# Output products of two FFN batches by blocks, seven for eight, in a fused attention and FFN kernel

## The chip, the cores and the metric

The kernel runs on one core of a Trainium2 chip. The metric is the device time of one execution in microseconds (us), as the median of several runs. The engines are called PE (TensorE; PEld is its weight load), DVE (VectorE), ACT (ScalarE), POOL (GpSimd) and SP (SyncE, which issues DMAs). PSUM is the memory that PE writes its sums to; SBUF is the other one.

## The reference

Four batches, four heads, 1088 tokens, head size 32. The attention is linear, with features phi; what follows works on 4352 tokens of 128 values and is bilinear:

```python
def phi(x):
    a = np.einsum('rd,bhsd->bhsr', S1, x)
    b = np.einsum('rd,bhsd->bhsr', S2, x)
    return np.einsum('bhsi,bhsj->bhsij', a, b).reshape(*x.shape[:-1], r * r)
q_p, k_p = (phi(q), phi(k))
kv = np.einsum('bhsf,bhsd->bhfd', k_p, v)
z = np.sum(k_p, axis=2)
num = np.einsum('bhsf,bhfd->bhsd', q_p, kv)
den = np.einsum('bhsf,bhf->bhs', q_p, z)[..., None] + 1e-06
...
a = x @ w1          # x: 4352 x 128, w1 and w2: 128 x 1024
b = x @ w2
h = a * b @ w3      # w3: 1024 x 1024
return (h @ w_out).astype(np.float32)   # w_out: 1024 x 128
```

All of it is in f32 in the kernel; `w3 @ w_out` is multiplied out first (w3o, 1024 x 128), so that per token there are two products into 1024 values, an elementwise product, and one product back to 128.

## The kernel before, in words

The work is cut into named steps. `make_steps` defines a function for each, and the string `ORDER` (L71) lists their names; each engine gets its instructions in the order of that list, as `tile_polysketch_attn__then__multiplicative_ffn_kernel` chains every instruction to the one before it on its engine. Semaphore waits between engines follow from the data. Buffers are placed by hand as well: `SLOTS` (L28) gives, kind by kind, which of a few places each next tile takes; kind "b" are the eight banks of PSUM, kind "m" are SBUF tiles of 128 x 512. A tile that takes a place waits for the last reader of the tile that had it. The sets `POOL`, `ACTS`, `CPV` and `CPG` (L51 to L66) say which engine runs a step: `on(name)` is POOL, ACT or else DVE, `cp(name)` is a copy on DVE if the name is in `CPV` and else on ACT.

The tokens are worked in groups of 512 (`g0` to `g7`, two for each batch) and a rest of 256 (`gr`). For g0 to g3 and the rest, `ffn` (L1685) does for each of eight chunks c of 128 of the 1024 values: product a (`a`), its copy to SBUF (`c`), product b (`b`), their elementwise product on DVE (`m`), and the product with w3o that adds chunk c to the output (`o`, L1732, or L1721 for the rest). Then the output is transposed in blocks of 32 on DVE (`oT`), for g4 to g7 scaled (`oS`), and stored by four DMAs (`st`).

The last two batches (groups 4 and 5, 6 and 7) get their products a and b from `seven` (L1604), named h4 and h6: the 128 inputs are halved (rows lo and hi of the array), the 1024 outputs are halved (chunk i and chunk i + 4), and the tokens are halved (group g and group g + 1). That is a product of 2x2 blocks by 2x2 blocks, done with seven products for eight (Winograd's form). A product uses 64 rows and 128 columns of the array; the `a` of a product lies on the lower 64 rows, the `b` on the upper 64, so two of them run side by side. For each of four i and for a and b there are products 1 to 7 into PSUM tiles X, Y and Z (L1644), copies c, d, e, i (ACT, L1651), additions f, g, h (DVE, L1656), and four elementwise products m11, m12, m22 (DVE or POOL, L1678) and m21 (DVE, L1683). The step names are like `h4.2b7`: pair h4, i = 2, weight b, product 7. The four blocks of the result are `ab_sb[g, i]`, `ab_sb[g, i + 4]`, `ab_sb[g + 1, i]`, `ab_sb[g + 1, i + 4]`. The sums of x that `seven` needs are s1 to s4, those of the weights v.1 to v.4 (POOL). The product with w3o is plain for these groups: 8 products of 128x128 with 512 tokens for each group.

x itself comes from `q_wide` (L1301): step `q4.x` (and q6.x, qr.x for the rest) multiplies into four PSUM banks of 256 tokens each, one for each quarter t of the batch. `seven` needs each half of x's rows on both halves of SBUF, so step `xTt` (L1525) copies the two halves k of a bank to both places u, four copies of 64 x 256; the even quarters go to ACT, the odd ones to DVE:

```python
eng = act.copy if t % 2 == 0 else dve.tensor_copy
for k in range(2):
    for u in range(2):
        eng(xd[key, t // 2][k][u * 64:u * 64 + 64, t % 2 * W:t % 2 * W + W],
            s["x"][t][k * 64:k * 64 + 64, :W])
```

In time, the last third of PE's order is: products o of g0 to g3; qr.x and q6.x; h4 (with the first four products of h6); the 16 products o of g4 and g5, with some of the rest's a and b between them; h6; the 16 products o of g6 and g7, again with the rest's; the rest's last products; its output.

Of the kernel before, what the change touches and what calls it, by code (L numbers as in the profile page):

```python
# [23 lines left out]
KIND = {"b": "out h kvz t wa wb", "l": "ph kp cv_m cv_c kh pT w3c w3T wv", "m": "hc xd nz t2 qT q2 s_hl xT ffa ab ay_C oT",  # L24
# [37 lines left out]
    g0.1c g0.3c g2.1c g2.5c g2.6c g3.4c gr.1c gr.4c k0.kT1 k1.kvc k2.kT1 k2.kq k3.kT0 k3.kT1 k3.kq  # L62
    q0.xc0 q0.xc1
# [50 lines left out]
h4.0b6 h4.1ac h4.0be h4.0ad q6.xT2 q6.xT3 h4.s4 h4.s3 h4.0bh h4.0a7 h4.0ag h4.1b5 h4.0a2 h4.0b3 h4.0a3 h4.0b7 v.4
h4.0a4 h4.2b1 h4.1bd h4.1a6 h4.1b3 h4.0ai h4.1ae h4.0ah h4.2bc h4.1a5 h4.1ad h4.0bg h4.0m11 h4.0bf h4.0m22 h4.0af
h4.0b4 h4.1a2 h4.2b2 h4.1a7 h4.1b1 h4.0m21 h4.0m12 h4.2bh h4.1ah h4.1a3 h4.3b1 h4.2a1 h4.1ag h4.1af h4.1bc h4.1b6
h4.2a2 h4.2ac h4.2ah h4.2b6 h4.1a4 q4.ns h4.1be h4.1b2 h4.1bh h4.1bf h4.3a1 h4.1ai h4.3ac h4.2be h4.3bc h4.1b7 h4.2a6
h4.3b5 h4.3a5 h4.1bg h4.3b2 h4.1m12 h4.3bh h4.3ad h4.2ae h4.3a6 h4.3ae h4.1b4 h4.1m21 h4.1m11 h4.3a3 h4.2m11 h4.3b6
h4.2a5 h4.2b7 h4.3bd h4.3af h4.2a7 h4.2b5 h4.3be h4.2ad h4.2a3 h4.3b7 h4.2bd h4.2ag h4.3a7 h4.2bg h4.3b3 h4.2af h4.2a4
h4.2b3 h6.1a1 h6.s1 h4.3ag h4.2b4 h4.3bf h4.2ai h4.2m21 h4.3a4 h4.3bg h6.0b1 h4.3a2 h4.2m22 h4.2bf h4.3ai h6.1b1  # L120
h4.3ah h4.3m22 h6.0a5 h4.3b4 h4.3m21 g5.0o g4.0o g5.4o g5.1o g4.4o g4.1o g4.5o g4.2o gr.1a h4.2m12 h4.1m22 g5.5o g5.2o
g5.6o h4.3m11 h4.3m12 gr.0a gr.0c h6.0ad h6.1bc gr.1c h6.0bc g5.3o g5.7o g4.6o gr.1b g5.oT gr.1m g4.3o g4.7o gr.0b
g4.oT h6.s2 h6.1b2 h6.s3 gr.0m h6.s4 h6.1bh h6.1a2 h6.1ac h6.0b2 h6.1a6 h6.1b5 h6.1ae h6.0bh h6.0a1 h6.1ah h6.1b6
# [18 lines left out]
def make_steps(ctx, tc, q, k, v, S1, S2, moe_w1, moe_w2, moe_w3, moe_w_out, out):  # L142
# [6 lines left out]
    NC = DF // 128  # L149
# [257 lines left out]
    w12 = consts.tile([128, 2, 2, 512], F32, tag="w12")  # L407
# [1424 lines left out]
```

## Time and profile before

| | us |
|---|---|
| median of three runs | 249.13 |
| the three runs | 248.73, 249.13, 250.8 |
| span of the profiled execution | 250.57 |
| PE busy | 241.0 (96%) |
| DVE busy | 192.1 (77%) |
| POOL busy | 124.5 (50%) |
| ACT busy | 117.5 (47%) |
| first product of h4 | 158.51 |
| last product of the rest starts | 246.79 |

The profiled execution is one run of its own; its span is near the slowest of the three. A row of the profile gives a line of the kernel, the engine, the operation, the tiles written and read, and how often; behind it the busy time and the mean length of one in ns, then the idle time of the engine ahead of it and what ended that. In a timeline the first two numbers are the start from the span's start and the length, in us. PE's products are pipelined: a product's row is longer than the time after which the next one starts. An f32 product has two rows, one for each of its two passes. In the windows, a stretch of time has the busy time of each engine and, in brackets, its instructions.

### The profile page before, as it was taken

The numbers are of one execution on the slowest core, as the hardware profiler recorded it, in microseconds if no ns is written. First come the engines' busy times: TensorE is split into PE (matmuls) and PEld (weight loads), VectorE is DVE, ScalarE is ACT, GpSimd is POOL, SyncE is SP. The second block draws the span as 40 slices with busy tenths as digits, with TensorE's granted clock in tenths as the row PEclk, the third lists the DMA queues.
The fourth block names the chain that finished last, engine by engine and source line by source line (L and its number), as shares of the span: only waits on it lengthen the run. The fifth ranks groups of instructions, "written<-read, shape, count | busy, mean of one in ns | idle before, by whom it ended". The sixth has DMA issues, their size and how long they took to land.

```text
span 250.6 us, 6584 instructions
## 1 busy us (share of the span) xinstructions
PE 241.0 (96%) x2678; PEld 143.0 (57%) x2678; DVE 192.1 (77%) x402; ACT 117.5 (47%) x234; POOL 124.5 (50%) x180
## 2 busy tenths in 40 slices
PE   8978999999999999999999999999999999999994
PEld 5867555545454645966566544476444567645474
DVE  2874889989899979898999898878992158878051
ACT  3975875755985564394000140785610337530020
POOL 4485455635739589735579747835230063520010
PEclk9997999999999999999999999999999999999999
DMA  7582969787879977000000000460000004000004
GB/s 197 186 221 88 299 166 192 154 219 180 233 172 219 217 196 186 15 4 0 3 0 0 4 0 0 73 100 0 1 0 0 0 7 79 0 1 0 3 12 93
DMA packets 31934, 22.06 MB, mean 88 GB/s; under 512 B 21280, under 2 KB 26528, under 8 KB 31904
## 3 DMA queue, kind: packets, MB, share of 16 engines
q1 hardware_dynamic: 31360, 21.11, 35.1%
q8 instruction: 21, 0.34, 0.6%
q10 hardware_dynamic: 544, 0.52, 0.6%
q14 instruction: 9, 0.07, 0.1%
HBM read 19.40 MB, written 2.23 MB: 86 GB/s over the span
## 4 chain that ended last, share of the span: by engine, by line
PE 78%; DVE 11%; DMA 4%; issue 2%; SPq 2%; ACT 1%; POOL 1%; DVEq 0%; ACTq 0%
PE ps_o L1732 22%; PE ps_X L1644 11%; PE a_ps L1697 9%; PE b_ps L1707 8%; PE ps_w3o L526 6%; PE ps_Y L1644 6%; PE ps_Z L1644 3%; DMA kr<-in_k_dram 2%; PE ps_ac L1366 2%; DVE ab L1713 2%; PE ps_kv L761 2%; PE ps_x L1519 2%; DMA k<-in_k_dram 2%; PE ps_g L651 1%; PE ps_or L1721 1%
## 5 line engine op out<-in xcount | busy, mean ns | idle before, releaser
L1644 PE MATMUL ps_X<-xd,wv 64*128 64x512 f32 x112 | 43.0, 596 | 0.3 <-issue 0.3
L1707 PE MATMUL b_ps<-xT,w 128*128 128x512 f32 (+1 forms) x80 | 36.9, 560 | 0.3 <-DVE ab L1713 0.2
L1702 ACT COPY ffa<-a_ps 128x512 f32<-128x512 f32 (+1 forms) x32 | 16.9, 547 | 41.4 <-PE a_ps L1697 41.3
L1697 PE MATMUL a_ps<-xT,w 128*128 128x512 f32 (+1 forms) x80 | 35.9, 556 | 0.0
L1651 ACT COPY hc<-ps_X 128x512 f32<-128x512 f32 x40 | 22.0, 595 | 18.8 <-PE ps_X L1644 18.0
L1732 PE MATMUL ps_o<-hc,w3o 128*128 128x512 f32 x64 | 29.3, 595 | 0.0
L1732 PE MATMUL ps_o<-ab,w3o 128*128 128x512 f32 x64 | 29.1, 595 | 0.0
L1713 DVE TENSOR_TENSOR ab<-ffa,b_ps 128x512 f32<-128x512 f32 (+1 forms) x40 | 24.0, 621 | 3.8 <-PE b_ps L1707 3.3
L493 POOL TENSOR_TENSOR w3c<-w3c,cv_m 128x512 int32<-128x512 int32 x16 | 21.0, 1326 | 6.3 <-DVE w3c L487 6.3
L1644 PEld LDWEIGHTS ps_X<-xd,wv 64*128 64x128 f32 x112 | 18.8, 186 | 8.6 <-issue 3.4
L1697 PEld LDWEIGHTS a_ps<-xT,w 128*128 128x128 f32 x80 | 14.5, 190 | 15.9 <-issue 10.9
L1644 PE MATMUL ps_Y<-xd,wv 64*128 64x512 f32 x48 | 23.2, 595 | 0.0
L1707 PEld LDWEIGHTS b_ps<-xT,w 128*128 128x128 f32 x80 | 13.9, 190 | 13.7 <-issue 9.4
L1732 PEld LDWEIGHTS ps_o<-ab,w3o 128*128 128x128 f32 x64 | 11.8, 190 | 13.7 <-issue 13.0
L1732 PEld LDWEIGHTS ps_o<-hc,w3o 128*128 128x128 f32 x64 | 12.0, 190 | 12.4 <-issue 11.3
L1739 DVE STREAM_TRANSPOSE oT<-ps_o 128x512 f32<-128x512 f32 x8 | 5.7, 715 | 16.9 <-PE ps_o L1732 16.6
L526 PEld LDWEIGHTS ps_w3o<-wo,w3T 128*128 128x128 f32 x128 | 15.3, 192 | 3.2 <-issue 2.5
L526 PE MATMUL ps_w3o<-wo,w3T 128*128 128x128 f32 x128 | 15.9, 277 | 0.6 <-DVE w3T L520 0.6
L1678 POOL TENSOR_TENSOR hc<-hc 128x512 f32<-128x512 f32 x7 | 8.8, 1275 | 13.3 <-DVE hc L1656 11.8
L530 ACT COPY w3o<-ps_w3o 128x128 f32<-128x128 f32 x8 | 2.1, 272 | 26.2 <-PE ps_w3o L526 26.2
L255 ACT ACTIVATE cv_c<-raw 128x1024 f32<-128x1024 f32 (+1 forms) x13 | 13.1, 1017 | 1.4 <-DMA raw<-in_moe_w_dram 1.4
L1656 DVE TENSOR_TENSOR hc<-hc,ps_Y 128x512 f32<-128x512 f32 x16 | 10.7, 682 | 4.0 <-ACT hc L1651 2.8
(316 smaller groups left out, 527.8 us busy)
## 6 DMA issues: line engine op xcount, KB each, us to landing
raw<-in_moe_w_dram SPq DMA_DIRECT2D x32, 256.0 KB, 5.1
qh<-in_q_dram SPq DMA_DIRECT2D x4, 544.0 KB, 4.0
raw<-in_moe_w_dram SPq DMA_DIRECT2D x4, 512.0 KB, 5.6
out_dram<-oT SPq DMA_DIRECT2D x32, 64.0 KB, 1.9
k<-in_k_dram SPq DMA_DIRECT2D x3, 512.0 KB, 4.2
v<-in_v_dram SPq DMA_DIRECT2D x2, 512.0 KB, 6.2
kh<-in_k_dram SPq DMA_DIRECT2D x8, 128.0 KB, 3.0
raw<-in_moe_w_out_dram SPq DMA_DIRECT2D x4, 256.0 KB, 5.5
```

What stands on the lines that cost most here:

```text
L255: act.activation(dst, hi.bitcast(F32), ACT.Prelu, scale=2.0 ** -112, alpha=-2.0 ** 32)
L493: pool.tensor_tensor(d, d, x["m"][:, i * 512:(i + 1) * 512], ALU.add)
L526: pe.matmul(t["o"], w3T[ko][:, c], wo[:, c], start=c == 0, stop=c == NC - 1)
L1644: pe.matmul(x[bank], stat(j, u)[:, i * 128:(i + 1) * 128], rows(j, u), start=new, stop=True, tile_position=(u * 64, 0), skip_group_check=True)
L1651: act.copy(x[k], x[bank])
L1656: dve.tensor_add(x[k], x[k], x[bank])
L1678: on(f"h{g}.{i}m{k}").tensor_mul(both[0][k], both[0][k], both[1][k])
L1697: pe.matmul(x["a"][:, :w], w_of(0, c), xT[g][:, c0:c0 + w], start=True, stop=True)
L1702: cp(f"g{g}.{c}{su}c")(x["s"][:, :w], x["a"][:, :w])
L1707: pe.matmul(x["b"][:, :w], w_of(1, c), xT[g][:, c0:c0 + w], start=True, stop=True)
L1713: dve.tensor_mul(ab_sb[g, c][:, c0:c0 + w], x["s"][:, :w], x["b"][:, :w])
L1732: pe.matmul(o_ps[g], w3o[:, c], ab_sb[g, c], start=c == turn[0], stop=c == turn[-1])
```

## The change

Three parts.

The output products of g4 and g5, and of g6 and g7, are made by blocks too. In `seven`, behind the elementwise products, steps T1 to T4 form four differences of blocks of the result for each i (on DVE or POOL), steps P1 to P7 are seven products of 128 rows and 64 columns, with 512 tokens each, 28 for a pair, and steps k1 to k9 put the two groups' outputs together from four PSUM banks (k1 a copy, k2 to k9 additions on DVE). P1, P2 and P6 lie on the left 64 columns, P4, P5 and P7 on the right, P3 left for i = 0 and 1 and right for i = 2 and 3. Steps o.S1 to o.S4 form the sums of w3o that P3, P5, P6 and P7 use (`ws`, 128 x 256 each, POOL). The 32 plain products go.

A quarter of x is copied three times: `xTt` copies all 128 rows of the bank to one tile, `xSt` (two copies of 64 x 256) the halves crosswise to the other. The upper half of the array then has the other half of x in each product, and `stat`, v.1 to v.4 change the weights to match.

`ORDER` is new from about its last third on, with other engines for some steps: the copies c, d, e, i can go to DVE, and seven of them do. The rest's products a and b move mostly behind the last P; qr.p01 and qr.phi0 go from POOL to DVE. q6.x is now ahead of qr.x. The stores are ordered g0, g2, g1, g3 where they were g3, g2, g0, g1.

The core of the diff:

```diff
 POOL = set("""
-    g4.oS g5.oS g6.oS h4.0m11 h4.0m12 h4.2m22 h4.s1 h4.s3 h4.s4 h6.0m22 h6.1m12 h6.1m22 h6.3m22 h6.s1
...
+    g4.oS g5.oS g6.oS h4.0T2 h4.0T3 h4.0T4 h4.0m11 h4.0m12 h4.1T2 h4.1T3 h4.1m12 h4.1m22 h4.2T1
+    h4.2T2 h4.2T4 h4.2m11 h4.3T3 h4.s1 h4.s2 h4.s3 h6.0T1 h6.0T2 h6.0T3 h6.0m12 h6.1T1 h6.1T2 h6.1T4
+    h6.1m11 h6.1m12 h6.2T4 h6.2m11 h6.2m12 h6.2m22 h6.3T2 h6.3T4 h6.s2 h6.s3 h6.s4 k0.Nf k0.Nh k0.Nr
...
 CPV = set("""
-    g0.1c g0.3c g2.1c g2.5c g2.6c g3.4c gr.1c gr.4c k0.kT1 k1.kvc k2.kT1 k2.kq k3.kT0 k3.kT1 k3.kq
-    q0.xc0 q0.xc1
+    g0.1c g0.3c g2.1c g2.5c g2.6c g3.4c h4.0ad h4.0be h4.1ac h4.1ae h6.1ai h6.1bd h6.3bd k0.kT1
+    k1.kvc k2.kT1 k2.kq k3.kT0 k3.kT1 k3.kq q0.xc0 q0.xc1 q4.xS1 q4.xT0 q4.xT1 q4.xT2 q4.xT3 q6.xS0
+    q6.xS1 q6.xS2
...
 ORDER = """
-g2.2o qr.rc qr.bs qr.phi0 q6.pT0 g1.oT g2.1o g2.7o q6.pT1 g3.7o qr.pT0 h4.s1 g2.oT g3.oT qr.x v.2 qr.xT0 q6.x h4.0a1
-h4.s2 h4.0b1 h4.1a1 q6.xT0 q6.xT1 h4.0b5 h4.0ac h4.0bc g3.st g2.st g0.st g1.st h4.0a6 h4.0b2 h4.0a5 h4.0bd h4.0ae
+q6.x v.2 q6.xT0 qr.x qr.xT0 q6.xS0 h4.0a5 q6.xT2 h4.0b1 h4.s2 q6.xS2 h4.0bc h4.s3 h4.0a1 h4.0b2 h4.1a1 h4.1b1 h4.0ac
+q6.xT1 h4.0a6 q4.ns h4.1bc q6.xS1 h4.s4 h4.0bh h4.0ad h4.0ae h4.1ac h4.0b6 h4.0a2 h4.1b6 h4.0b5 v.4 h4.1a6 h4.0be
...
+h4.1T4 h4.3bf h4.3a3 h4.2m21 h6.3bc h4.0T2 h4.3a4 h4.3b4 gr.5a h4.3af h4.1P5 h4.1P6 h4.3bh
...
+h4.2T1 h4.2P5 h4.2P2 h4.3T2 h4.3T4 h4.0P1 h4.1P7 h4.0T4 h4.1P4 h4.3P1 h4.0P4 h4.2T2 h4.0P6 h4.2P6 h4.2T3 h6.s1 h4.3T3
...
+h4.2P3 h6.0b1 h6.0bc h6.0a5 h6.0ad h4.k3 h4.k2 h4.k4 h4.k5 h6.0b5 h4.k7 h4.k8 g3.st h4.k6 h6.0a6 h6.0ae h4.k9 h6.s4
...
+h6.3T2 h6.3T4 gr.5m h6.1P7 h6.3P2 h6.0P1 h6.3P5 h6.3P7 h6.3P1 h6.k1 h6.0T4 h6.3P4 h6.2T4 h6.1T4 h6.2P6 h6.0P4 h6.3P6
+h6.k2 q6.ns h6.0P3 gr.6m h6.k3 h6.k4 h6.k5 h6.k7 h6.1P4 h6.2P4 h6.1P3 gr.1a gr.6o0 gr.1b gr.0a gr.5o0 gr.6o1 gr.1c
...
@@ q_wide
-                    eng = act.copy if t % 2 == 0 else dve.tensor_copy
+                    cp(nm(f"xT{t}"))(quarter(xd[key, t // 2][0], t % 2), s["x"][t][:, :W])
+
+                @step(nm(f"xS{t}"))
+                def _(t=t):
                     for k in range(2):
-                        for u in range(2):
-                            eng(xd[key, t // 2][k][u * 64:u * 64 + 64, t % 2 * W:t % 2 * W + W],
-                                s["x"][t][k * 64:k * 64 + 64, :W])
+                        cp(nm(f"xS{t}"))(quarter(xd[key, t // 2][1], t % 2)[64 - k * 64:128 - k * 64],
+                                         s["x"][t][k * 64:k * 64 + 64, :W])
...
@@ seven
-                        act.copy(x[k], x[bank])
+                        cp(n(y))(x[k], x[bank])
...
+        B11, B12, B21, B22 = (lambda i, t=t, c=c: ab_sb[g + t, i + c] for t, c in ((0, 0), (1, 0), (0, 4), (1, 4)))
...
+                on(f"h{g}.{i}T1").tensor_sub(y[1, i], B12(i), B11(i))
...
+                on(f"h{g}.{i}T2").tensor_sub(y[2, i], B22(i), y[1, i])
...
+                on(f"h{g}.{i}T3").tensor_sub(y[3, i], B22(i), y[3, i])
...
+                on(f"h{g}.{i}T4").tensor_sub(y[4, i], y[2, i], B21(i))
+
+            low, high = (0, 64), (64, 128)
+            for j, (bank, half, w, x) in {
+                1: (0, low, lambda i: w3o[:, i, :64], B11),
+                2: (2, low, lambda i: w3o[:, i + 4, :64], B21),
+                3: (3, high if i // 2 else low, lambda i: ws[0][:, 3, i], B22),
+                4: (2, high, lambda i: w3o[:, i + 4, 64:], lambda i: y[4, i]),
+                5: (1, high, lambda i: ws[0][:, 0, i], lambda i: y[1, i]),
+                6: (1, low, lambda i: ws[0][:, 1, i], lambda i: y[2, i]),
+                7: (0, high, lambda i: ws[0][:, 2, i], lambda i: y[3, i]),
+            }.items():
+                @step(f"h{g}.{i}P{j}")
+                def _(i=i, j=j, bank=bank, half=half, w=w, x=x):
+                    if bank not in acc_o:
+                        acc_o[bank] = ps("out", [128, 512], "ps_o")
+                    n = seen_o[bank, half] = seen_o.get((bank, half), 0) + 1
+                    pe.matmul(acc_o[bank][half[0]:half[1]], w(i), x(i), start=n == 1, stop=n == (2 if j == 3 else 4),
+                              tile_position=(0, half[0]), skip_group_check=True)
...
+            cp(f"h{g}.k1")(y["s"][lo], acc_o[0][lo])
...
+            dve.tensor_add(o_sb[g][lo], y["s"][lo], acc_o[2][lo])
+
+        put("k2", k2)
+        put("k3", lambda: dve.tensor_add(y["s"][hi], y["s"][lo], acc_o[1][lo]))
+        put("k4", lambda: dve.tensor_add(o_sb[g][hi], y["s"][hi], acc_o[0][hi]))
+        put("k5", lambda: dve.tensor_add(o_sb[g + 1][hi], o_sb[g][hi], acc_o[1][hi]))
+        put("k6", lambda: dve.tensor_sub(o_sb[g][hi], o_sb[g][hi], acc_o[2][hi]))
+        put("k7", lambda: dve.tensor_add(y["s"][hi], y["s"][hi], acc_o[1][hi]))
+        put("k8", lambda: dve.tensor_add(o_sb[g + 1][lo], y["s"][hi], acc_o[3][hi]))
+        put("k9", lambda: dve.tensor_add(o_sb[g + 1][lo], o_sb[g + 1][lo], acc_o[3][lo]))
...
@@ ffn
-                    if c == turn[0]:
-                        o_ps[g] = ps("out", [128, 512], "ps_o")
-                    pe.matmul(o_ps[g], w3o[:, c], ab_sb[g, c], start=c == turn[0], stop=c == turn[-1])
...
-                dve.transpose(oT[0], o_ps[g])
+                dve.transpose(oT[0], o_sb[g] if whole else o_ps[g])
```

In the new kernel the P steps are line 1759, T1 to T4 are lines 1727, 1732, 1737 and 1742, the products of `seven` are line 1673, the block copies line 1680, the block additions line 1685, and k1 to k9 lie between lines 1767 and 1785.

More of the change, by code (lines that the diff above doesn't have):

```diff
@@ L114 @@
[L114 to L123, printed above, removed]
@@ new lines, in seven, with _, put, k2 @@
+        lo, hi = slice(0, 64), slice(64, 128)
+        @step(f"h{g}.k1")
+        def _():
+            y["s"] = sb("oc", [128, 512], name="oc")
+            cp(f"h{g}.k1")(y["s"][lo], acc_o[0][lo])
+        def put(name, f):
+            @step(f"h{g}.{name}")
+            def _():
+                f()
+        def k2():
+            o_sb[g], o_sb[g + 1] = (sb("oc", [128, 512], name="oc") for _ in range(2))
+            dve.tensor_add(o_sb[g][lo], y["s"][lo], acc_o[2][lo])
+        put("k2", k2)
@@ L1718, in _ @@
                     def _(c=c, u=u):
-                        if c == 0:
+                        if (g, u) not in o_ps:
                             o_ps[g, u] = ps(("out", "kvz")[u], [128, DM], "ps_or")
+                        n = seen[g, u] = seen.get((g, u), 0) + 1
                         pe.matmul(o_ps[g, u], ab_sb[g, c][:, u * DM:(u + 1) * DM], w3o[:, c],
-                                  start=c == 0, stop=c == NC - 1)
+                                  start=n == 1, stop=n == NC)
         if g != "r":
-            first = {}
-            turn = [c for i in range(4) for c in (i, i + 4)] if whole else range(NC)
-            for c in range(NC):
-                @step(f"g{g}.{c}o")
-                def _(c=c):
-                    if c == turn[0]:
-                        o_ps[g] = ps("out", [128, 512], "ps_o")
-                    pe.matmul(o_ps[g], w3o[:, c], ab_sb[g, c], start=c == turn[0], stop=c == turn[-1])
+            if not whole:
+                for c in range(NC):
+                    @step(f"g{g}.{c}o")
+                    def _(c=c):
+                        if g not in o_ps:
+                            o_ps[g] = ps("out", [128, 512], "ps_o")
+                        n = seen[g] = seen.get(g, 0) + 1
+                        pe.matmul(o_ps[g], w3o[:, c], ab_sb[g, c], start=n == 1, stop=n == NC)
             oT = {}
```

111 lines of the change are left out of this document (78 added, 33 removed).

## The prediction

> **What bounds the kernel now.** I read the page first, then its 40 slices, then the last third stage by stage.
>
> ```profile
> span 250.6 us, 6584 instructions
> PE 241.0 (96%) x2678; PEld 143.0 (57%) x2678; DVE 192.1 (77%) x402; ACT 117.5 (47%) x234; POOL 124.5 (50%) x180
> PE   8978999999999999999999999999999999999994
> DVE  2874889989899979898999898878992158878051
> ```
>
> TensorE is busy in every slice; VectorE leaves two holes, around 194 us and from 230 us on, which are the stages of plain output products that the change rewrites. The windows cut the last third at the first product of the batch pair h4 (158.51), at the first g5.0o (185.62), at the first remaining product of h6 (201.28), at g7.0o (224.20), and at the end of the last array slot (246.90).
>
> ```profile
> 158.51:185.62 27.11, 26.78 (x125) 15.04 (x120) 22.86 (x39) 17.86 (x36) 13.64 (x26) 1.00 0.23 37
> 185.62:201.28 15.66, 15.66 (x42) 7.52 (x40) 5.59 (x11) 2.33 (x5) 0.00 (x0) 1.00 0.00 0
> 201.28:224.20 22.92, 22.92 (x105) 15.02 (x104) 16.95 (x28) 12.34 (x23) 11.37 (x24) 1.00 0.14 24
> 224.20:246.90 22.70, 22.70 (x90) 14.12 (x88) 11.18 (x22) 2.26 (x6) 1.05 (x1) 1.00 0.11 18
> 246.90:250.57 3.67, 0.17 (x2) 0.00 (x0) 0.00 (x0) 0.27 (x1) 0.00 (x0) 0.90 0.32 72
> ```
>
> Columns: length, then busy time of PE, weight loads, DVE, ACT and POOL, granted clock (1.00), DMA share, GB/s. "Busy" does not say that the array is full, so I compare with its floor. Every f32 product is two instructions (passes).
>
> ```profile
> 234.67 3.60 PE L1732 MATMUL ps_o<-hc,w3o 128*128 128x512 f32 x8
> 238.11 0.59 PE L1697 MATMUL a_ps<-xT,w 128*128 128x256 f32 x2
> 238.54 1.02 PE L1732 MATMUL ps_o<-hc,w3o 128*128 128x512 f32 x2
> ...
> 177.26 0.59 PE L1644 MATMUL ps_Y<-xd,wv 64*128 64x512 f32 x1
> 177.27 0.59 PE L1644 MATMUL ps_X<-xd,wv 64*128 64x512 f32 x1
> 177.69 0.59 PE L1644 MATMUL ps_Y<-xd,wv 64*128 64x512 f32 x1
> 177.70 0.59 PE L1644 MATMUL ps_X<-xd,wv 64*128 64x512 f32 x1
> ```
>
> Eight full passes take 238.11 - 234.67 = 3.44 us, 0.43 each, though a row says 0.59. A pass on half the rows also takes 0.43, and the two halves run at once. Two 256-column passes take 238.54 - 238.11 = 0.43, so a gr product of 256 columns costs 0.43 and one of 128 columns 0.215. The floor from 158.51 on: 112 half-row products at two per 0.86 (48.1), 32 full ones at 0.86 (27.5), 16 gr a/b at 0.43 (6.9), 16 gr o at 0.215 (3.4): 85.9. Measured to 246.90: 88.4. Only some 2.6 us are waits (with the unrounded 0.4288), of which 0.8 lie in the first stage's start. So the array's slots set the end, and the change attacks them. But all of it is at most the slots saved, and each new wait is paid in full.
>
> **The change, part by part.**
>
> *Slots.* Each pair loses 16 full products and gets 28 of 128x64. Whether two such halves run together has a row in this kernel, four passes of one quarter's x:
>
> ```profile
> L1289 PE MATMUL ps_x<-pT,kz x4: 592/618/643, 45.4 to 45.9; 128*64 128x512 f32 x4
> 45.44 1.08 PE L1289 MATMUL ps_x<-pT,kz 128*64 128x512 f32 x4
> ```
>
> Two products, four passes, in 1.08 us: one alone would take 0.43 + 0.59 = 1.02. They run together. So 14 slots for 16, 2 x 0.86 per pair: **-3.44 us**. Every half product is used: 14 on the left and 14 on the right in each pair (P3 lies left for two blocks, right for two).
>
> *Three copies for four.* Of the two batches, 32 copies of 64x256 become 8 of 128x256 and 16 of 64x256.
>
> ```profile
> 158.62 3.49 DVE L1532 COPY xd<-ps_x 64x256 f32<-64x256 f32 x8 [0.96 <-PE ps_x L1519]
> 158.62 1.50 ACT L1532 COPY xd<-ps_x 64x256 f32<-64x256 f32 x4 [0.86 <-issue]
> L1702 DVE COPY ffa<-a_ps 128x256 f32<-128x256 f32 x2 | 0.8, 406 | 3.9 <-PE a_ps L1697 3.9
> L1702 ACT COPY ffa<-a_ps 128x256 f32<-128x256 f32 x6 | 2.0, 376 | 28.0 <-PE a_ps L1697 28.0
> ```
>
> Eight copies at about 0.4 go, 3.2 us spread over two engines, none of them the bound: worth 0 in itself. What counts is the order. Before, h4's first products did not need the second batch's copies. Now the first one, h4.0a5, waits for q6.xT0 (ACT) and then q6.xS0 (two DVE copies), which free its PSUM place.
>
> ```profile
> 156.26 2.32 PE L1519 MATMUL ps_x<-pT,kq 32*32 32x64 f32 x128
> 158.51 0.69 PE L1644 MATMUL ps_X<-xd,w 64*128 64x512 f32 x1
> 158.52 0.69 PE L1644 MATMUL ps_X<-xd,wv 64*128 64x512 f32 x1
> 159.91 0.59 PE L1644 MATMUL ps_X<-xd,w 64*128 64x512 f32 x1
> 160.83 0.66 PE L1644 MATMUL ps_X<-xd,wv 64*128 64x512 f32 x1 [0.33 <-issue]
> 160.84 0.69 PE L1644 MATMUL ps_Z<-xd,w 64*128 64x512 f32 x1
> L1651 ACT COPY hc<-ps_X 128x512 f32<-128x512 f32 x40 | 22.0, 595 | 18.8 <-PE ps_X L1644 18.0
> L1656 DVE TENSOR_TENSOR hc<-hc,ps_Y 128x512 f32<-128x512 f32 x16 | 10.7, 682 | 4.0 <-ACT hc L1651 2.8
> ```
>
> (The last two rows give the copy and the addition of a block, 0.60 and 0.68 us.)
>
> q6.x now runs first and is done near 157.75 (an estimate: 156.26 plus two thirds of the x products' 2.3 us); 0.4 for xT0, 0.9 for xS0 and the hand-overs: h4 starts near 159.2, 0.7 late. Then, on ACT, q6.xT1 stands behind the copies h4.0bc and h4.0ac. 0ac needs product 0a1, second on its half: it ends at 159.2 + 2 x 0.86 + 0.16 = 161.1. So xT1 runs at 161.6, and DVE's q6.xS1, which waits for it, at 162.05; behind it on DVE stand s4, 0bh, 0ad and 1ac (0.9 + 4 x 0.6): 1ac is done near 165.5, and h4.1a6 needs it. By then that half has run five products, 4.3 us since 159.2: it stands 2.0 us. The other half stands with it: at 160.83 a product that had waited starts, and only at 160.84 the next one on the other half, free since 160.34 (159.91 + 0.43). Together 2.7 against the 0.8 lost there before: **+1.9 us**. Bounds: 0 if xT1 is early after all; 3 if 0ah, next on DVE, also delays 1b2.
>
> *T and k steps, ws.* 32 differences T (14 DVE, 18 POOL), 16 additions k2 to k9 on DVE, two copies k1 on ACT; four POOL sums ws. VectorE also takes over seven copies from ACT and gives four products m to POOL.
>
> ```profile
> 177.60 1.29 DVE L1678 TENSOR_TENSOR hc<-hc 128x512 f32<-128x512 f32 x2
> L1678 POOL TENSOR_TENSOR hc<-hc 128x512 f32<-128x512 f32 x7 | 8.8, 1275 | 13.3 <-DVE hc L1656 11.8
> ```
>
> DVE issues one per 0.61 (1.29 - 0.68), so 14 + 16 + 7 - 4 = 33 add some 20 us to the 56.6 in the windows: 76 of 88. POOL gets 22 more of 1.27 and ws at about half of that (256 columns), 31 us on 26. Neither passes TensorE in sum. In detail, h4's end: behind product 3a3 DVE has 3af, 3bh, 2m12, 3m11, 3m21, 3m12, 2m22, 3T1, 3m22, 3T2 and 3T4, 11 steps or 7.1 us with the last three chained; 3P4, the 16th of the 28, starts 0.86 + 0.43 (gr.5a) + 0.2 (switches) + 14 x 0.43 - 0.16 = 7.3 us behind 3a3's end. It holds by 0.2. The start of h6: k3 can go 2.4 us ahead of the end of P, and k2 to k9, some of them chained, fill eight times 0.65, up to 2.8 us behind it; then 0ah, done at 3.5. The sixth product on its half, 1a5, is the first that needs 0ah, at 0.1 + 5 x 0.86 = 4.4. The products that take over P's PSUM places need k4, k7, k6 and k9, each 0.2 us or more ahead of its turn. So zero in both places, with margins that rival 2 uses up.
>
> At the end of h6 one wait is not covered. k2 reads PSUM place 2 after 0P4, and 1P4 and 2P4, which write there, wait for k2. All three are on the right half. 0P4 ends at s + 1.02, k2 takes 0.7, so 1P4 starts at s + 1.8 instead of s + 0.86; only 3P6 and 0P3, on the left, lie beside it: **+0.95 us**. In h4 the same step has other products ahead: 0. gr.1a then waits for k4: k3 and k4 end 2.0 us behind k2, near the end of 2P4 and 1P3: 0, bounds 0 to 0.5.
>
> *Switches between row halves, full array and column halves.* Three before, six now.
>
> ```profile
> 200.76 0.59 PE L1707 MATMUL b_ps<-xT,w 128*128 128x256 f32 x2
> 201.28 0.69 PE L1644 MATMUL ps_Z<-xd,w 64*128 64x512 f32 x1
> 201.29 0.69 PE L1644 MATMUL ps_Z<-xd,wv 64*128 64x512 f32 x1
> ```
>
> The two passes end their slots at 201.19; the next starts at 201.28: 0.1 each. **+0.3 us** (to 0.5).
>
> *Tail.* The last store leaves SP behind eight issues of g6 and g7.
>
> ```profile
> 242.83 4.18 SPq L1548 DMA_DIRECT2D out_dram<-oT  x8
> 247.40 0.62 SPq L1554 DMA_DIRECT2D out_dram<-oT  x1
> ```
>
> 0.52 an issue. After k9, g7's transposition (0.72), gr.4m (0.37) and scaling (0.68) end near 2.3 us before the last gr product; four issues take 2.1. Just covered: 0, up to 1 if DVE slips. The stores of g0 to g3 go earlier; g4's must land before h6.2bd and 2bg reuse their places, about 0.4 us of margin: 0.
>
> Sum: -3.44 + 1.9 + 0.95 + 0.3 = **-0.3 us**. The profiled execution spans 250.6, close to the slowest of the three runs (250.8); the median is 249.13. I take the difference from the median: **248.8 us**.
>
> **The rivals.**
>
> 1. *The slots come through.* If the start loses no more than before (q6's copies out of the way) and the k2 wait is as worked out: -3.44 + 0.95 + 0.3 = -2.2, 246.9; without the k2 wait 246.0. For it: the same first products were ready at 158.5 before. Against it: the queue order above.
>
> 2. *VectorE becomes the bound in h6* (the slower side). From h4's k3 to h6's k4 it has 61 instructions in about 40.1 us (36.4 of slots, the 2.4 from above, 0.3 of switches, 0.95): it decides once the mean interval passes 40.1 / 61 = 0.66. At the 0.68 of a step that waits for its predecessor (T and k are such chains) 61 x 0.68 = 41.5, +1.4; with T2 and T4 bouncing to POOL at 1.27, another 1 to 2. That gives 250.2 to 252.2. For it: DVE at 0.61 has a margin under 10%. Against: products, not VectorE, ended most waits in its rows.
>
> 3. *A half used twice running costs a pass.* The new order has 35 places where two neighbours use the same half (6, 7, 14 and 8 in its four half-array stretches); the old has none. If passes had to start strictly in program order, each would cost 0.43: 15 us, 260.5. Against it: at 177.26 and 177.27 both halves start, and the first passes of L1289's two products lie within its first 0.1 us, so the second product does not wait for the first one's second pass.
>
> The Trainium skill ("TensorE: Matmul & The Clock Gate", Part 3, The mechanism) states that matmuls start and end in strict program order; read pass by pass, that rule is rival 3, with 260.5. The rows agree with it only product by product, and by that the repeats cost nothing but what is in my sum.
>
> **How the numbers follow.** My sum 0.51, rival 1 0.20, rival 2 0.25, rival 3 0.04. The likeliest case's own range, from the bounds of start (-1.9 to +1.1) and end (-0.5 to +1), is 247.3 to 250.5; the range of 246.0 to 252.0 takes in rivals 1 and 2. One per cent is 2.5 us, about what a measurement tells from no change: faster than 246.6 needs rival 1 nearly whole, 0.16; slower than 251.6 is half of rival 2, rival 3 and a little of mine, 0.21; within, 0.63.
>
> **What would show it.** 56 passes of L1759, 128*64, in 12.0 us in h4: the slots. A first h4 product about 0.7 later than q6.x's end allows, and a gap of over 1 us on the half of 1a6, released by DVE: the start; without it rival 1. A right half standing 0.9 us ahead of 1P4 and released by DVE's k2. DVE idle under 1 us between k3 and the next k4: rival 2. Starts 0.86 apart where a half repeats, with the other half idle: rival 3. The forecast is wrong if the products wait on something other than these queues.

## The result, and the profile after

The changed kernel takes 262.0 us (four runs, 260.9 to 263.6); the kernel before took 249.97 beside it. The ratio is 1.047 (95% interval 1.040 to 1.055): slower by 12 us, where 248.8 was forecast and no value above 252 was held likely. Two of the four runs of the kernel with all of it on VectorE, and the profiled run of the one with fills, are slower executions at a granted clock of 0.98 to 0.99, and the ratios leave them out.

The head of the page of the profiled execution after:

```profile
span 259.1 us, 6749 instructions
...
PE 245.1 (95%) x2726; PEld 133.9 (52%) x2726; DVE 223.5 (86%) x431; ACT 114.9 (44%) x227; POOL 159.3 (61%) x204
...
PE   8999888999999999999999998898996999999994
...
DVE  3779879998999888988998885998998899899792
...
PE 59%; DVE 27%; issue 6%; POOL 5%; ACT 1%; DVEq 0%; ACTq 0%; POOLq 0%
```

VectorE has no hole left (86% busy, 77 before), and it is the second in the chain that ended last, with 27%. The windows of the last third, cut at h4's first product, its half-array stretch, h6's first product, its half-array stretch, and the rest's own products (columns as in the prediction):

```profile
157.40:187.50 30.10, 28.30 (x116) 13.37 (x116) 26.12 (x40) 14.81 (x29) 19.74 (x29) 1.00 0.13 22
187.50:203.74 16.24, 14.11 (x61) 4.51 (x59) 14.45 (x17) 1.69 (x4) 11.63 (x8) 1.00 0.00 1
203.74:228.54 24.80, 24.34 (x110) 11.44 (x109) 23.80 (x38) 12.02 (x22) 13.03 (x12) 1.00 0.13 21
228.54:246.20 17.66, 17.19 (x64) 5.59 (x63) 15.95 (x21) 1.54 (x3) 12.10 (x20) 1.00 0.00 1
246.20:255.30 9.10, 9.07 (x56) 8.25 (x56) 7.48 (x15) 2.14 (x6) 1.88 (x6) 1.00 0.30 48
```

In the second window PE is idle for 2.1 us, in the fourth for 0.5, and in both it is less than full beyond that: 56 half passes, of 28 products (with two or six short passes of the rest ahead of them), take 16.2 and 17.7 us, and their slots are 12.0. From h4's first product to the last slot (the start of the last pass) it is 97.9 us, against 88.3 before. The floor of slots fell as forecast, by 3.4, from 85.65 to 82.22, but what the array loses over its floor rose from 2.6 to 15.7. (The profiled spans differ by 8.5 us only, as the stretch ahead of h4 was 1.1 us shorter in this execution.) This table has the length of each stretch in us, cut at the starts of its first product and of the one behind its last; a pass of a half is 0.43 us, two run at once. The last four columns are kernels of the experiments.

| stretch (passes) | floor | after | one-input | one-input, early start | other division | replanned, scale later |
|---|---|---|---|---|---|---|
| h4 rows (116) | 24.9 | 30.13 | 28.41 | 25.99 | 29.32 | 25.55 |
| h4, P1 to P7 (56) | 12.0 | 15.58 | 12.16 | 12.17 | 13.59 | 12.34 |
| h6 rows (108) | 23.2 | 24.80 | 24.07 | 24.06 | 24.80 | 23.52 |
| h6, P1 to P7 (56) | 12.0 | 16.18 | 13.28 | 13.28 | 14.71 | 13.25 |
| over the floor in all | | 15.7 | 6.9 | 4.5 | 11.4 | 3.5 |

The two longest waits of the products P for another engine in the last third (waiting instruction, what ended its wait, total, times, longest):

```profile
PEld ps_o L1759 <- DVE tt L1742: 3.4, 2, 2.8
PEld ps_o L1759 <- DVE hc L1737: 2.8, 3, 1.2
```

L1742 is T4, L1737 is T3: the steps that the prediction had costed at nothing. Their rows, with those of the products m (L1707), T1 (L1727) and an addition that reads PSUM (L1685), first before (m alone), then after:

```profile
L1678 DVE TENSOR_TENSOR hc<-hc 128x512 f32<-128x512 f32 x17 | 11.1, 686 | 0.0
```

```profile
L1707 DVE TENSOR_TENSOR hc<-hc 128x512 f32<-128x512 f32 x13 | 13.3, 1038 | 0.1
L1685 DVE TENSOR_TENSOR hc<-hc,ps_Y 128x512 f32<-128x512 f32 x16 | 10.8, 676 | 0.0
L1737 DVE TENSOR_TENSOR hc<-hc 128x512 f32<-128x512 f32 x4 | 5.9, 1482 | 0.1
L1727 DVE TENSOR_TENSOR tt<-hc 128x512 f32<-128x512 f32 x5 | 5.4, 1088 | 0.1
L1742 DVE TENSOR_TENSOR tt<-tt,hc 128x512 f32<-128x512 f32 x3 | 4.0, 1339 | 0.0
```

The same instruction took 0.686 us before and 1.04 to 1.48 on the mean after, where both of its inputs lie in SBUF (VectorE's two T2, which are not among these rows, took 0.69). With one input in PSUM it takes 0.68 in both kernels. The two engines side by side, VectorE first (start, length):

```profile
191.58 1.28 DVE L1707 TENSOR_TENSOR hc<-hc 128x512 f32<-128x512 f32 x2
...
193.38 1.75 DVE L1707 TENSOR_TENSOR hc<-hc 128x512 f32<-128x512 f32 x1
195.17 0.69 DVE L1732 TENSOR_TENSOR tt<-hc,tt 128x512 f32<-128x512 f32 x1
195.90 1.63 DVE L1742 TENSOR_TENSOR tt<-tt,hc 128x512 f32<-128x512 f32 x1
197.45 1.75 DVE L1737 TENSOR_TENSOR hc<-hc 128x512 f32<-128x512 f32 x1
```

```profile
193.00 1.58 POOL L1732 TENSOR_TENSOR tt<-hc,tt 128x512 f32<-128x512 f32 x1 [2.49 <-DVE hc L1707]
195.28 1.70 POOL L1737 TENSOR_TENSOR hc<-hc 128x512 f32<-128x512 f32 x1 [0.69 <-DVE hc L1707]
196.95 1.72 POOL L1742 TENSOR_TENSOR tt<-tt,hc 128x512 f32<-128x512 f32 x1
```

At 191.58 GpSimd is idle: two products in 1.28. The one that begins at 193.38 ends at 195.13, and GpSimd's step ends at 194.58: VectorE's ends 0.55 behind it, so nearly all of its own 0.68 lies behind GpSimd's end. At 195.28 GpSimd meets VectorE's step of 195.17 and takes 1.70 for 1.27; VectorE's step of 195.90 then ends at 197.53, again 0.55 behind GpSimd's end at 196.98. They take turns. Added up over the 30 such steps of VectorE from 153 us on, 15 are slowed, to at most 1.76, by 12.2 us in all; no step with an input in PSUM took more than 0.693.

### The profile page after: what moved, and what is told of

Read it like the earlier page. It is cut to its first block, busy times and chain, and to the rows that moved or that the text cites. A ratio compares the mean times of both kernels' runs of the same rounds, so it can differ in the third digit from the quotient of the medians.

```text
span 259.1 us, 6749 instructions
## 1 busy us (share of the span) xinstructions
PE 245.1 (95%) x2726; PEld 133.9 (52%) x2726; DVE 223.5 (86%) x431; ACT 114.9 (44%) x227; POOL 159.3 (61%) x204
## 4 chain that ended last, share of the span: by engine, by line
PE 59%; DVE 27%; issue 6%; POOL 5%; ACT 1%; DVEq 0%; ACTq 0%; POOLq 0%
PE ps_o L1835 11%; PE a_ps L1799 8%; PE b_ps L1809 8%; PE ps_w3o L536 6%; PE ps_o L1759 4%; PE ps_X L1673 4%; DVE hc L1707 4%; DVE hc L1685 4%; PE idle_ps L257 3%; PE ps_g L661 2%; PE ps_ac L1376 2%; POOL hc L1707 2%; DVE ab L1815 2%; PE ps_x L1529 2%; PE ps_Y L1673 2%
## 5 line engine op out<-in xcount | busy, mean ns | idle before, releaser
L1673 PE MATMUL ps_X<-xd,wv 64*128 64x512 f32 x96 | 34.2, 601 | 0.1
L1673 PE MATMUL ps_Y<-xd,wv 64*128 64x512 f32 x64 | 29.0, 603 | 1.4 <-ACT xd L1539 0.8
L1680 ACT COPY hc<-ps_X 128x512 f32<-128x512 f32 x36 | 20.2, 590 | 22.4 <-PE ps_X L1673 13.3
L1804 ACT COPY ffa<-a_ps 128x512 f32<-128x512 f32 (+1 forms) x34 | 17.8, 535 | 23.3 <-PE a_ps L1799 23.2
L1707 POOL TENSOR_TENSOR hc<-hc 128x512 f32<-128x512 f32 x11 | 14.7, 1351 | 7.9 <-DVE hc L1685 7.9
L1673 PEld LDWEIGHTS ps_X<-xd,wv 64*128 64x128 f32 x96 | 13.1, 186 | 9.5 <-issue 5.1
L1673 PE MATMUL ps_Z<-xd,wv 64*128 64x512 f32 x32 | 16.8, 608 | 0.0
L1759 PE MATMUL ps_o<-hc,w3o 128*64 128x512 f32 x32 | 15.3, 601 | 0.0
L1759 PE MATMUL ps_o<-hc,ws 128*64 128x512 f32 x32 | 14.7, 598 | 0.4 <-DVE hc L1737 0.3
L1673 PEld LDWEIGHTS ps_Y<-xd,wv 64*128 64x128 f32 x64 | 10.4, 186 | 9.0 <-issue 3.8
L1673 PE MATMUL ps_X<-xd,w 64*128 64x512 f32 x32 | 12.5, 602 | 1.5 <-DVE hc L1685 1.5
```

The source lines that it names most:

```text
L1673: pe.matmul(x[bank], stat(j, u)[:, i * 128:(i + 1) * 128], rows(j, u), start=new, stop=True, tile_position=(u * 64, 0), skip_group_check=True)
L1680: cp(n(y))(x[k], x[bank])
L1707: on(f"h{g}.{i}m{k}").tensor_mul(both[0][k], both[0][k], both[1][k])
L1759: pe.matmul(acc_o[bank][half[0]:half[1]], w(i), x(i), start=n == 1, stop=n == (2 if j == 3 else 4), tile_position=(0, half[0]), skip_group ...
L1804: cp(f"g{g}.{c}{su}c")(x["s"][:, :w], x["a"][:, :w])
```

## The experiments

**One input for VectorE's steps.** Theory A: the two engines shut each other out. Theory B: VectorE just has too many steps. Theory C: the prediction's third rival, repeats of a half, which happened to give the time that came out.

```diff
+    def two(name, op, dst, p, q, keep):
+        if on(name) is pool:
+            getattr(pool, op)(dst, p, q)
+        else:
+            dve.transpose(dst, (p, q)[keep])
...
-                    on(f"h{g}.{i}m{k}").tensor_mul(both[0][k], both[0][k], both[1][k])
+                    two(f"h{g}.{i}m{k}", "tensor_mul", both[0][k], both[0][k], both[1][k], 1)
```

and so for T1 to T4.

> Theory A (VectorE and GpSimd stand in each other's way): in the trace of the changed kernel the VectorE steps that read two SBUF tiles (products m, differences T) take 1.2 to 1.76 us where a GpSimd step runs beside them and 0.68 where none does; those that read PSUM take 0.68 always. The excess adds up to some 12 us. Here those VectorE steps are transpositions of one of their two inputs (the profile has 0.70 for such a one); GpSimd's steps, the counts and the order stay. The kernel leaves out VectorE's share of the products m and differences T. A: all of these rows at 0.70, GpSimd's T and m back at 1.28, and 252 to 256 us. Theory B (VectorE simply has too many steps, at one per 0.61): 262, as the count is the same. Theory C (a half of the array used twice running costs a pass): 262.

Measured: 251.2 us, a little under A's 252, ratio to the kernel before 1.005 (1.001 to 1.009), so some 10 us of the 12 are gone. The row of VectorE's 17 transpositions for m and T3, and that of GpSimd's m and T3:

```profile
L185 DVE STREAM_TRANSPOSE hc<-hc 128x512 f32<-128x512 f32 x17 | 11.4, 689 | 0.2
```

```profile
L183 POOL TENSOR_TENSOR hc<-hc 128x512 f32<-128x512 f32 x15 | 18.9, 1286 | 7.6 <-DVE hc L1691 7.6
```

Of VectorE's 27 transpositions 19 run beside a GpSimd step that reads, and none takes more than 0.712. The counts are the same on both engines, so B and C fall: what cost the time is the second SBUF input. (A step with one input also waits for one tile less; the other division below, which leaves nothing out, has no such difference.) With the T's in time, the half-array stretch of h6 shows the repeats too:

```profile
228.79 0.59 PE L1765 MATMUL ps_o<-tt,ws 128*64 128x512 f32 x1
228.79 0.59 PE L1765 MATMUL ps_o<-hc,w3o 128*64 128x512 f32 x1
229.22 0.59 PE L1765 MATMUL ps_o<-hc,ws 128*64 128x512 f32 x1
229.22 0.59 PE L1765 MATMUL ps_o<-tt,ws 128*64 128x512 f32 x1
...
233.94 0.59 PE L1765 MATMUL ps_o<-tt,w3o 128*64 128x512 f32 x1
233.94 0.59 PE L1765 MATMUL ps_o<-tt,ws 128*64 128x512 f32 x1
```

Both halves start together, 0.43 apart, 13 times from 228.79 to 233.94, though the order repeats a half on the way; the stretch of h4, with seven repeats, takes 12.16. Taken two by two, the products of these stretches always use both halves: all 15 repeats lie between such pairs.

**No T at all.** P4 to P7 read the blocks themselves:

```diff
-                on(f"h{g}.{i}T1").tensor_sub(y[1, i], B12(i), B11(i))
+                pass
...
-                5: (1, high, lambda i: ws[0][:, 0, i], lambda i: y[1, i]),
+                5: (1, high, lambda i: ws[0][:, 0, i], B11),
```

> The 32 differences T are left out and P4 to P7 read blocks of the elementwise product instead, so nothing but products m stands ahead of a P. A and B: most of the 13 us that the array lost more than before goes, 251 to 254 us, and the stretch of 56 half products in h4 falls from 15.6 to 12.0 to 12.8. C: that stretch has 7 repeats of a half and the one in h6 has 8; it would stay above 15, and the time above 258.

Measured: 253.6 us (ratio 1.014, 1.007 to 1.021); h4's P stretch 12.17, h6's 14.45. C is out by its own numbers. The run doesn't tell A from B, and the 2.4 us by which it is behind the run before are in part its m, which still meet: VectorE's 13 take 0.79 on the mean.

**All of it on VectorE.**

```diff
-    g4.oS g5.oS g6.oS h4.0T2 h4.0T3 h4.0T4 h4.0m11 h4.0m12 h4.1T2 h4.1T3 h4.1m12 h4.1m22 h4.2T1
+    g4.oS g5.oS g6.oS h4.s1 h4.s2 h4.s3 h6.s2 h6.s3 h6.s4
```

> All T and all m of both pairs on VectorE, the same order. VectorE gets 29 more steps (17.7 us at 0.61) and loses the 12.4 us of standing behind GpSimd. A: every such row at 0.69 and about the same time, 259 to 266. B: the 17.7 us come on top of a bound VectorE, 272 or more. C: 262.

Measured: 269.7 us (265.9 to 270.3; ratio 1.070, 1.058 to 1.081).

```profile
L1701 DVE TENSOR_TENSOR hc<-hc 128x512 f32<-128x512 f32 x24 | 16.0, 685 | 0.1
L1731 DVE TENSOR_TENSOR hc<-hc 128x512 f32<-128x512 f32 x8 | 5.5, 685 | 0.0
```

The rows are as A said, 0.685. The fastest run lies within A's range, the other three above its 266, and all below B's 272. How much of the excess is the kernel's is open: the granted clock was 0.981 to 0.987 in these runs, and in the traced one it was 0.90 and 0.91 in the two P stretches, which is worth up to 3.4 us. But VectorE's plain load does bind with these 29 steps more: in h6's rows, at a clock of 1.00, it is busy for 27.3 of 27.5 us, and the stretch was 24.8 in the changed kernel. So GpSimd's help is needed, and only its coincidence with VectorE's two-input steps is the harm.

**The start undone.** `q6.xT1 q6.xS1` directly behind `q6.xS0`:

```diff
-q6.xS0 h4.0a5 q6.xT2 h4.0b1 h4.s2 q6.xS2 h4.0bc h4.s3 h4.0a1 h4.0b2 h4.1a1 h4.1b1 h4.0ac q6.xT1 h4.0a6 q4.ns h4.1bc q6.xS1 h4.s4
+q6.xS0 q6.xT1 q6.xS1 h4.0a5 q6.xT2 h4.0b1 h4.s2 q6.xS2 h4.0bc h4.s3 h4.0a1 h4.0b2 h4.1a1 h4.1b1 h4.0ac h4.0a6 q4.ns h4.1bc h4.s4
```

> Only the start of h4 is undone: q6.xT1 and q6.xS1 stand directly behind q6.xS0, ahead of the copies 0bc and 0ac on ScalarE and of s4, 0bh, 0ad and 1ac on VectorE. If the prediction's step is right (2.0 us of standing before 1a6), the array loses 1.0 instead of 2.7 in h4's first 8 us and the time falls by 1.5 to 2.0, to about 260.2. Rival: the wait only moves to another copy (0ac and 0bc now come 0.6 later each): no gain, 262.

Measured: 258.0 us (ratio 1.031, 1.025 to 1.037), 2.9 to 4 under the changed kernel by the ratios, more than the 1.5 to 2.0 expected. In its trace the array loses 0.3 us in h4's first 8 us, for 2.6, and h4's rows are 2.4 us shorter (27.73). The P stretch behind them is 1.7 longer (17.27), but not by a wait: the wait for T4 ahead of its second half is the same in the changed kernel (first two rows) and here (the next two); then the clock granted to TensorE is halved and passes start 0.83 to 0.86 apart. In the window, 0.50 is that clock.

```profile
197.58 0.64 PE L1759 MATMUL ps_o<-tt,w3o 128*64 128x512 f32 x1 [1.88 <-DVE tt L1742]
198.06 0.59 PE L1759 MATMUL ps_o<-tt,w3o 128*64 128x512 f32 x1
```

```profile
193.35 1.04 PE L1759 MATMUL ps_o<-tt,w3o 128*64 128x512 f32 x1 [1.87 <-DVE tt L1742]
194.18 1.06 PE L1759 MATMUL ps_o<-tt,w3o 128*64 128x512 f32 x1
194.00:196.00 2.00, 2.00 (x8) 0.59 (x6) 1.57 (x2) 0.00 (x0) 0.71 (x2) 0.50 0.00 0
```

So the late start cost the array 2.4 us. What the medians gained beyond that is not located, and may lie in the part ahead of h4, which differs by some 2 us between single executions of these kernels.

**The changed kernel again, other divisions, and a GpSimd that reads nothing.**

> The changed kernel once more, so that the next kernels stand beside it on one chip: 260 to 263 us, and again VectorE steps of 1.2 to 1.76 us where two SBUF tiles are read beside a GpSimd step.

Measured: 260.9 us (ratio 1.043, 1.037 to 1.048). The other division, as names that leave the set POOL and come to it:

```diff
-    h4.0T4 h4.0m12 h4.2T1 h4.2T2 h4.2T4 h4.3T3 h6.1T1 h6.1T4 h6.2T4 h6.3T4
+    h4.1m11 h4.2m22 h4.3m22 h6.2T1
```

> Order and counts as in the changed kernel; only ten of the 29 T and m steps on GpSimd go to VectorE (h4.0T4, 0m12, 2T1, 2T2, 2T4, 3T3; h6.1T1, 1T4, 2T4, 3T4) and four come back (h4.1m11, 2m22, 3m22; h6.2T1), chosen so that fewer of them run beside two-input steps of VectorE. Theory A (the two engines exclude each other while both read SBUF twice or at all): some 4 to 5 of the 12.4 us of standing go and VectorE's six more steps of 0.61 take 3.7 back only where it is the bound: 256 to 259 us. Theory B (VectorE's number of steps is the bound): 3.7 us slower, 265 to 266. Theory C (repeats of a half): unchanged, 262.

Measured: 255.5 us (ratio 1.023, 1.019 to 1.027), 5.4 less with six steps more on VectorE and just under A's 256: B has the wrong sign. The slowed steps fell from 15 to 9 and what they lost from 12.2 to 6.3 us: 5.9 less standing, 5.4 less time. GpSimd's share as fills, which read nothing (against the helper `two` of the first experiment; VectorE does its own operations again):

```diff
+            pool.memset(dst, 0.0)
-            getattr(pool, op)(dst, p, q)
```

> As the changed kernel, but GpSimd's 18 T and 11 m are a fill of the same tile with zero: GpSimd writes 128x512 and reads nothing, and its steps wait for less. The kernel leaves out GpSimd's share of the products m and differences T. If the exclusion is over the reading of SBUF: VectorE's two-input steps at 0.68 everywhere and about the time of the run with one-input steps, 249 to 252 us. If any GpSimd work on SBUF hinders them: rows above 1.0 us stay, and 255 or more. B and C: 262, but for what GpSimd's own waits were worth, 260.

Measured: 251.3 us (ratio 1.006, 1.002 to 1.010). The traced execution lost 5 us ahead of h4, so only rows are read from it: VectorE's m (and T3), and GpSimd's fills.

```profile
L185 DVE TENSOR_TENSOR hc<-hc 128x512 f32<-128x512 f32 x17 | 11.3, 683 | 0.1
```

```profile
L183 POOL MEMSET hc<- 128x512 f32 x15 | 7.6, 523 | 24.7 <-DVE tt L185 13.2 <-DVE hc L1691 11.6
```

VectorE reads its two SBUF tiles at full speed beside writes of GpSimd: five of its 27 such steps met a fill and took 0.68 to 0.69. The fills are also shorter and wait for less, so this run alone would not prove it; with the first one it does: the harm needs two SBUF inputs on VectorE's side and reading on GpSimd's.

**The last third planned anew.** The changed kernel with early xT1 and xS1, and with the order and the division of steps chosen from the durations of the rows, VectorE's two-input steps being made to wait for GpSimd's and the other way round. The work is whole. The names of the two pairs that leave the set POOL and come to it, and the order at the start of h4's P stretch (the scaling of one group also leaves POOL and that of another comes, and eleven copies change their engine):

```diff
-    h4.0T2 h4.1T2 h4.1m12 h4.1m22 h4.2T1 h4.2T2 h4.2T4 h4.3T3 h4.s3 h6.1T1 h6.1T2 h6.2m22 h6.3T2 h6.3T4
+    h4.0m22 h4.1T1 h4.1T4 h4.1m11 h4.2m12 h4.2m22 h4.3m22 h6.0m11 h6.1T3 h6.1m22 h6.2T1 h6.3T3
...
-gr.5a h4.3af h4.1P5 h4.1P6 h4.3bh h4.2m12 h6.0ac h4.0P2 h4.0P5 h4.3m11 h4.3ai h4.1T3 h4.3m21 h4.3m12 h4.1P1
+gr.5a h4.3af h4.1P5 h4.1P6 h4.0P6 h4.3bh h4.0P2 h4.1P4 h4.0P4 h4.3m11 h4.3m21 h4.3T1 h4.1P1 h4.0P7 h4.1P7
```

> The changed kernel with q6.xT1 and q6.xS1 early, and with the last third's order and the division of T, m and copies over the engines chosen anew so that VectorE's two-input steps fall where GpSimd is idle (28 T and m on GpSimd). The work is all there. A: floor of the array's slots 82.3 plus the k2 wait, three to six switches and a start of 0.8 as in the kernel before: 86 to 87 from h4's first product to the last slot, against 97.9; 249 to 251 us on the clock of the changed kernel's 262, at best 1 per cent under the kernel before. B: VectorE's number of steps is hardly less, 258 or more. C: the half-array stretches stay long, 258 or more.

Measured: 250.0 us (ratio 1.001, 0.999 to 1.004), and 87.15 from first product to last slot, for 86 to 87 expected. The slowed steps lose 2.3 us. 2.87 of the 4.94 over the floor fell in the last P stretch:

```profile
226.93 5.52 POOL L1491 COPY nz<-nz 32x8 f32<-32x8 f32 x16
232.54 2.49 POOL L1734 TENSOR_TENSOR tt<-tt,hc 128x512 f32<-128x512 f32 x2
```

> As the replanned kernel before it, which took 87.15 us from h4's first product to the last slot and lost 2.87 of its 4.94 us in the last half-array stretch, where h6's T4 stood on GpSimd behind q6.ns (16 small copies of nz, 226.93 to 232.45). Now order and division are chosen with 5.5 us for such a group, so that no T waits for it. A: those 2 to 2.5 us go, 84.5 to 85.5 from first product to last slot, 247.5 to 248.3 us, faster than both kernels. Rival: other collisions of two-input steps with GpSimd take their place, 250.

Measured: 251.6 us (ratio 1.005, 1.002 to 1.009): a miss. The rival held: its rows of h4 take 26.98 and 13.09 for the 25.55 and 12.34 of the kernel before it, and the group of copies now stood beside VectorE's two-input steps and took longer still:

```profile
225.31 7.80 POOL L1491 COPY nz<-nz 32x8 f32<-32x8 f32 x16
```

So the first plan was kept, and one step moved in it:

```diff
-h6.3T3 q6.ns h6.1T4 h6.2T4
+h6.3T3 h6.1T4 h6.2T4 q6.ns
```

(GpSimd's order alone.)

> The first replanned kernel (250.0, 87.15 us from h4's first product to the last slot) with one step moved: q6.ns, 16 small copies on GpSimd, goes behind h6.1T4 and h6.2T4. There it stood from 226.2 to 232.5 ahead of these two, whose inputs VectorE had ready by 229.95; they ended at 235.03 and the last two pairs of passes waited for them. Now they run from about 229.9 to 232.4, before their products' turn: the 2.87 us lost in that stretch fall by 2.0 to 2.6, 247.4 to 248.0 us, under the kernel before by 0.7 to 1 per cent. Rival: the 16 copies now delay the scaling of g6 and its stores at the end, and half of it or more is lost again, 249 to 250.

Measured: 248.85 us, ratio 0.997 (0.994 to 0.9995): under the kernel before, barely, and the fastest with all the work in it. The expected 2.0 to 2.6 came to 1.6 in that stretch (14.88 to 13.25) and to 1.2 in the medians: T4's two steps end at 231.57, where they were expected (this execution is 0.7 ahead of the other one throughout). What is still lost in that stretch, 1.25 us, was not traced further.

```profile
228.69 2.88 POOL L1734 TENSOR_TENSOR tt<-tt,hc 128x512 f32<-128x512 f32 x2 [3.16 <-DVE tt L1724]
...
231.80 3.56 POOL L1491 COPY nz<-nz 32x8 f32<-32x8 f32 x16
```

**Both causes away in the change's own order.**

> The changed kernel with one-input steps on VectorE (its share of m and T left out, as in the first experiment) and with q6.xT1 and q6.xS1 early (as in the fourth): what the change is worth in its own order without the exclusion and without the late start. The first alone gave 251.2; its array lost 6.9 us, of which 2.65 in h4's first 8 us. If both causes simply add: 251.2 - 1.7 to 2.0 = 249.3, the time of the kernel before. If the late start was hidden under something else once the exclusion is gone: 251.

Measured: 248.97 us (ratio 0.999, 0.994 to 1.004), 2.2 under the first experiment, or 1.5 by the two ratios (the two were measured on different chips, and the kernel before took 250.26 here for 249.55). The array's loss over its floor falls by 2.4: the causes add, and without them the change is worth nothing that can be measured against the kernel before. In its trace 4.5 us over the floor are left (2.6 before), and 0.8 ahead of h4's first product, where TensorE did not stand before; so of the 3.4 us of slots only 0.8 is left.

## Why the prediction was wrong, step by step

*What bounds the kernel* held for the kernel before and failed for the one after: the array's slots fell by 3.4, and then the array waited.

*Slots, -3.44*: right. 28 half products take 12.16 us where nothing holds them up.

*Start, +1.9*: right in place, too small. The prediction's 2.7 us against 0.8 before were a first product 0.7 late and 2.0 of standing behind it. The first product did stand, 0.8 us, and the half of 1a6 stood 1.96 us, from 162.25, when the pass of 161.82 has left its slot, to 164.21, when VectorE's copy 1ac is done, with xS1 late behind xT1:

```profile
157.39 0.67 PE L1673 MATMUL ps_Y<-xd,wv 64*128 64x512 f32 x1 [0.81 <-ACT xd L1539]
...
161.82 0.59 PE L1673 MATMUL ps_X<-xd,wv 64*128 64x512 f32 x1
...
164.21 1.12 PE L1673 MATMUL ps_X<-xd,wv 64*128 64x512 f32 x2
```

```profile
160.28 0.86 DVE L1544 COPY xd<-ps_x 64x256 f32<-64x256 f32 x2 [1.99 <-ACT xd L1539]
161.06 1.18 DVE L1659 TENSOR_TENSOR xd<-xd 128x512 f32<-128x512 f32 x1
```

But with the waits of the other half the array lost 2.6 us in h4's first 8 us, for 0.7 before; with the 0.8 ahead of them that is +2.7, 0.8 more than the term. Of these, 0.5 are s4, behind xS1: it reads two SBUF tiles and took 1.18 beside GpSimd's v.4. Taken away on its own (the last experiment against the first) the standing was worth 2.4 in the array.

*k2 at the end of h6, +0.95*: right. The right half stands from 243.28, when the pass of 242.84 has left its slot, to 244.37, 1.09 us, beside VectorE's k2 (L1776):

```profile
242.84 0.59 PE L1759 MATMUL ps_o<-tt,w3o 128*64 128x512 f32 x1
...
243.28 1.02 PE L1759 MATMUL ps_o<-hc,ws 128*64 128x512 f32 x2
244.37 0.61 PE L1759 MATMUL ps_o<-tt,w3o 128*64 128x512 f32 x1
```

```profile
243.54 0.68 DVE L1776 TENSOR_TENSOR oc<-oc,ps_o 64x512 f32<-64x512 f32 x1 [1.27 <-PE ps_o L1759]
```

*T and k steps, 0*: this is the step that failed. It said "DVE issues one per 0.61" and "Neither passes TensorE in sum", and gave 3P4 a margin of 0.2 us. The 0.61 came from rows of the kernel before in which VectorE never read two SBUF tiles while GpSimd worked on such a step: its 17 m and GpSimd's seven in the last third don't overlap in time once. The rows to compare were the times of both, not the means. The change brought 32 more steps of that kind and split them over the two engines, so that 15 of VectorE's were slowed. That is the 10 us between the changed kernel and the first experiment (ratios 1.043 to 1.047 against 1.005; 8.8 us of the array's time in the two traces). Rival 2 had the engine right, VectorE, but asked at what mean interval it would become the bound (0.66) and only in h6; the interval grew where two engines met, in both P stretches, and the time came out 10 us above the rival's 252.

The Trainium skill states what is seen here ("SBUF — State Buffer", Who interferes with whom): a VectorE instruction with two SBUF inputs contends with a GpSimd instruction that reads SBUF, not with one that only writes it, and the one that comes second is blocked until the first is done. The trace agrees on all three: 1.75 us beside a reading step of GpSimd, ended 0.55 behind that step's end; 0.68 to 0.69 beside fills; 0.676 with an input in PSUM. It was the rule that spoke against this change, and the prediction had weighed another.

*Switches and tail*: the tail lost 0.6 behind the last P, after and in the first experiment alike; both terms together are too small to be told apart.

*Rival 3* gave 260.5 and the time is 262, but its mechanism is not there, and the nearness is chance: seven repeats cost 0.16 us in h4's stretch of the first experiment, where it charged 3.0. (Nor does 260.5 follow from its terms: 15 us on the sum's 248.8 are 263.8.) The first replanned kernel goes further: its h4 stretch has 15 repeats, ten of them inside such a pair, and takes 12.34 us. There 0P2 on the left half stands ahead of 1P4 on the right in `ORDER`, and 1P4 starts at 184.78 and 0P2 at 185.63.

*The likeliest case's range*, 247.3 to 250.5, does not follow from its own bounds either (added to 248.8 they give 246.4 to 250.9), which changes nothing here: the time lies far outside both.

What stays open: why taking away the start alone gave 2.9 to 4 us in the medians and 2.4 in the array, and how much of the time with all steps on VectorE is the clock's.

## What to carry to other kernels

Before a step is given to GpSimd, or a two-input SBUF step added to VectorE, list in time which steps of the other engine run beside it; a mean from a trace in which the two never met says nothing of the case where they do. A step that reads PSUM on one side is free of it, so such steps are the ones to lay beside GpSimd's. And a margin of 0.2 us on a chain whose durations are borrowed from another schedule is no margin.

## What the runs showed of the hardware that was not expected

VectorE's addition or product of two 128x512 f32 tiles of SBUF took up to 1.76 us for 0.69 when it met a GpSimd step, and GpSimd's up to 1.73 for 1.27. Sixteen copies of 32x8 on GpSimd took 3.56 us in the kernel planned last, where they met none of VectorE's two-input steps, 5.52 in the first replanned one, where they met five, and 7.80 in the second, where they met ten: about 0.4 us for each, while these steps of VectorE took 0.68 to 0.73. A fill of 128x512 on GpSimd took 0.52 us. Products of 64 columns on the two halves of the array kept 0.43 us a pass in each, also where the order has the same half several times running. And the clock granted to TensorE was halved for 3.4 us at a time in some executions: once in h4's P stretch with the early start (1.7 us), once in each P stretch with all steps on VectorE.
